# First batch of a spectral filter and its MLP on one core: filter rows in both partition halves, two load queues, another order of loads and sums

## The chip, the core and the metric

The kernel runs on one core of a Trainium2 chip. The metric is the time on the device in microseconds (us), from the program's start to its end: the median of three runs of the kernel before is 2878.39 us (2875.7 to 2886.1). The profile is one execution of it, with a span of 2877.8 us.

## The reference, cut to what matters

```python
batch, seq, dim = (8, 3008, 256)          # x; filt_r and filt_i have seq // 2 + 1 = 1505 rows
X = np.fft.rfft(x, axis=1)
y = np.fft.irfft(X * (filt_r + 1j * filt_i)[None], n=seq, axis=1)
# then each of the 8 * 3008 = 24064 rows of y, as a token of 256 numbers:
h = y @ w_in                              # 256 x 2048
g = h - np.tanh(h)
out = g @ w_out                           # 2048 x 256
```

The two weight matrices come as 64-bit floats; all else is float32.

## The kernel before

A transform of 3008 = 64 x 47 points is done in matmuls. Per batch there are four steps, with a trip through DRAM between them, because each step has another index in the partitions:

1. `first`: a 64-point transform. `x` is loaded, multiplied by `wf1` into PSUM (`pf`), copied by ACT (`a1`) and stored to `ct1`.
2. `middle`: 32 frequency slots, each a 47-point transform. `a2` comes from `ct1`; the matrices of four slots (`fg`) come in one load (`load_slots`); the product `pz` is multiplied by the filter (`fr` and `fi`), transformed back (`pe`), copied (`e1`) and stored to `ct2`.
3. `last`: the 64-point inverse. `e2` comes from `ct2`, and the product `pu` holds tokens, feature by token.
4. `up`, `shrink`, `down`: the MLP on groups of up to 512 tokens, in a form with seven products for eight. It needs sums and differences of weight blocks, made by POOL (G).

The batches go in units (0), (1, 2), (3, 4), (5, 6), (7). In the long main loop, `first` and `middle` of the next unit lie between the MLP steps of the present one. Unit 0 has nothing to hide behind: it is done in a part of its own, which this text calls the prologue. There the weights of five of the eight weight quarters are also converted from 64-bit words to float32 (`weights`), two jobs to a quarter, each in two stages with a `yield` after each, so that they are strung between the other steps.

Each engine issues its instructions in the order of the text, within each `manual_schedule` region. So an instruction that waits holds up all later ones of its engine, and a load that waits for its buffer holds up all later loads of its queue. SP issues most loads, ACT the stores of `a1` and `e1`, POOL the loads of the filter in the prologue.

The prologue, shortened (cuts are marked with `# ...`):

```python
nc.sync.dma_start(wf1, wf1_d)
xs = [load_x0(0, (0, 4, 8))]                 # x in three chunks of 8 of 24 steps
ws = weights(tiles0, range(5), 3)            # 10 jobs, 3 raw loads ahead; "raw" has 3 buffers
xs += [load_x0(1), load_x0(2)]
# ... pad to ct1
fts = {0: filters_of(0)}                     # POOL: memset, then 6 loads of filter rows
# ... gx cleared
next(ws)                                     # the first 3 raw loads
for c in range(3):
    for k, _ in enumerate(first0(xs[c], c)): # matmuls pf, ACT copies a1, ACT stores
        if k == 3 or k == 1 and c > 0:
            next(ws)                         # one stage of a weight job
G.dma_start(s2, s2_d)
fts[1] = filters_of(1)
a2 = {0: load_a2(0, 0, False)}
mats = {0: load_slots(0, pro), 1: load_slots(1, pro)}
next(ws)
double_filters(fts[0], 0)
turned(mats[0][1], gx[0])
for j in range(NK // 2):                     # 16 steps of two slots, c = j // 2
    # at even j: load a2[c + 1], mats[c + 2], fts[c + 2]
    # pz: 4 matmuls; back0 of step j - 1: 8 matmuls pe, ACT copy e1, store to ct2
    V.tensor_mul(uv, pz, ft[:, 0])
    V.tensor_mul(zs, pz, ft[:, 1])
    next(ws, None)
    # at odd j: double_filters and turned for c + 1
    if j == NK // 2 - 2:
        fs = first(1, z1)
        next(fs)                             # the first two x loads of unit 1
back0()
for _ in ws:
    pass
e2s[0] = load_e2(*groups[0])                 # all tokens of the first group
```

and what these call:

```python
def load_x0(c, cuts=(0, 8)):
    t = big([128, 8, DM], F32, "x0")
    for lo, hi in zip(cuts, cuts[1:]):
        for _, rows, r, n in halves(0, 8 * c + lo, hi - lo):   # partitions 0 to 63, then 64 to 127
            nc.sync.dma_start(t[rows, lo:lo + n, :], ...)

def filters_of(c, to=None):                  # t = filt[c % 3], [128, 2, 4, 256]
    # ... memset of t[32:64]
    for v, src in enumerate((filt_r, filt_i)):
        for row, m in ((0, LO), (LO, 16), (LO + 16, HI - 16)):  # 24, 16 and 7 partitions
            put(row, m, v, 0, n, src, ...)   # t[row:row + m, v, ...]: partitions 0 to 46

def double_filters(t, c):                    # partitions 64 to 127 get what 0 to 63 hold
    for v in range(2):
        ACT.copy(t[IM:128, v], t[0:IM, v])   # IM = 64

def weights(tiles, quarters, ahead):         # its loop over jobs k
    next(began[k])                           # stage 1: four DVE and two ACT operations on raw
    if k + ahead < len(jobs):
        began.append(start(k + ahead))       # SP: a raw load of 512 KB
    yield
    next(began[k])                           # stage 2: DVE writes wu or wd
    if k % 2:
        # four G.tensor_sub on the quarter just done
    yield
```

After the prologue, the main loop opens with `last` of group 0 (`pu`), and strings the 24 steps of `first` of unit 1, one x chunk each, between the MLP steps of unit 0.

Of the kernel before, what the change touches and what calls it, by code (L numbers as in the profile page):

```python
# [37 lines left out]

UNITS = [(0,), (1, 2), (3, 4), (5, 6), (7,)]
HALF = (NR + 1) // 2  # L40


def steps_of(unit):
# [97 lines left out]
def kernel(  # L141
# [81 lines left out]
    def weights(tiles, quarters, ahead):  # L223


        jobs = []
        for k in quarters:
            u = k % 4
            for h in range(2):
                if k < 4:  # L230
                    cols = slice(256 * u, 256 * u + 256)
                    src = bass.AP(tensor=moe_w_in.tensor, offset=128 * h * DFF + 256 * u,
                                  ap=[[DFF, 128], [DFF // 2, 2], [1, 256]])
                    dsts = [(slice(0, 256), wu[:, (0, 1)[h], cols], 1.0),
                            (slice(256, 512), wu[:, (6, 3)[h], cols], (1.0, -1.0)[h])]
                else:
                    t = 2 * u + h
                    cols = slice(128 * t, 128 * t + 128)
                    src = bass.AP(tensor=moe_w_out.tensor, offset=128 * t * DM,
                                  ap=[[DM, 128], [DFF // 2 * DM, 2], [1, DM]])  # L240
                    dsts = [(slice(0, 256), wd[:, 0:7:6, cols], 1.0),
                            (slice(256, 384), wd[:, 1, cols], 1.0),
                            (slice(384, 512), wd[:, 3, cols], -1.0)]
                jobs.append((src, dsts))

        def start(k):
            j = converted(tiles, *jobs[k], nc.sync)
            next(j)
            return j

        began = [start(k) for k in range(ahead)]
        yield
        for k in range(len(jobs)):
            next(began[k])
            if k + ahead < len(jobs):
                began.append(start(k + ahead))
            yield
            next(began[k])
            if k % 2:
                u = quarters[k // 2]  # L260
                w = (wu if u < 4 else wd)[:, :, 256 * (u % 4):256 * (u % 4) + 256]
                G.tensor_sub(w[:, 4], w[:, 6], w[:, 3])
                G.tensor_sub(w[:, 5], w[:, 4], w[:, 0])
                G.tensor_sub(w[:, 2], w[:, 1], w[:, 5])
                G.tensor_sub(w[:, 6], w[:, 0], w[:, 6])
            yield

    def halves(p, r, n):

# [132 lines left out]

    CHUNKS = [chunks_of(bs, CH) for bs in UNITS]

    def load_e2(p, c):
        r, n = CHUNKS[p][c]
        t = tr.tile([128, CH, DM], F32, tag="e2", bufs=2, name="e2")
        if len(UNITS[p]) == 2:
            nc.sync.dma_start(t[:, 0:n, :], dram(ct2[p], r * DM, [[RP * DM, 128], [1, n * DM]]))
        else:  # L410
            for _, rows, r_h, n_h in halves(p, r, n):
                nc.sync.dma_start(t[rows, 0:n_h, :],
                                  dram(ct2[p], r_h * DM, [[RP * DM, 64], [1, n_h * DM]]))
        return t
# [323 lines left out]
    psums = []  # L738

    def z1(name, shape):  # L740
        return psums[0].tile(shape, F32, tag="t", bufs=1, name=name)

    with tc.tile_pool(name="tr", bufs=2) as tr:
        with tc.tile_pool(name="pro", bufs=1) as pro, \
                tc.tile_pool(name="ps0", bufs=6, space=bass.MemoryType.PSUM) as ps0:

            def z0(name, shape):
                return ps0.tile(shape, F32, tag="z", bufs=6, name=name)

            def big(shape, dtype, name):  # L750

                return pro.tile(shape, dtype, tag="big", bufs=4, name=name)

            def load_x0(c, cuts=(0, 8)):
                t = big([128, 8, DM], F32, "x0")
                for lo, hi in zip(cuts, cuts[1:]):
                    for _, rows, r, n in halves(0, 8 * c + lo, hi - lo):
                        nc.sync.dma_start(t[rows, lo:lo + n, :],
                                          dram(x.tensor, r * DM, [[NR * DM, 64], [1, n * DM]]))
                return t  # L760

            def first0(xt, c):
# [24 lines left out]
            def filters_of(c, to=None):  # L787


                n = 4 if c < NK // 4 - 1 else 3  # L790

                def put(row, m, v, i, n_s, src, off, dims):
                    if to is None:
                        dst = t[row:row + m, v, i:i + n_s, :]
                    else:
                        dst = dram(to, ((row * 2 + v) * NK + 4 * c + i) * DM,
                                   [[2 * NK * DM, m], [DM, n_s], [1, DM]])
                    (G if to is None else nc.sync).dma_start(dst, dram(src.tensor, off, dims))

                if to is None:  # L800
                    t = filt[c % 3]


                    if c < 3:
                        G.memset(t[32:64], 0.0)
                    if n == 3:
                        G.memset(t[0:1, 1, 3], 0.0)
                for v, src in enumerate((filt_r, filt_i)):
                    for row, m in ((0, LO), (LO, 16), (LO + 16, HI - 16)):
                        sign = 1 if row < LO else -1  # L810
                        r0 = 4 * c + 1 + NQ * row if row < LO else NQ * (row - LO + 1) - 1 - 4 * c
                        put(row, m, v, 0, n, src, r0 * DM,
                            [[NQ * DM, m], [sign * DM, n], [1, DM]])
                    if n == 3:
                        put(v, LO - v, v, 3, 1, src, v * NQ * DM,
                            [[NQ * DM, LO - v], [DM, 1], [1, DM]])
                        put(LO, HI, v, 3, 1, src, NQ // 2 * DM,
                            [[NQ * DM, HI], [DM, 1], [1, DM]])
                return None if to is not None else t

            def double_filters(t, c):
                for v in range(2):
                    ACT.copy(t[IM:128, v], t[0:IM, v])
                if c == NK // 4 - 1:
                    ACT.dma_start(t[IM:IM + 1, 0, 3, :],
                                  dram(filt_r.tensor, SEQ // 2 * DM, [[DM, 1], [1, DM]]))
# [17 lines left out]
            with tc.manual_schedule():  # L844
                nc.sync.dma_start(wf1, wf1_d)
                V.memset(near_b, B)
                V.memset(exp_b, -896.0)
                xs = [load_x0(0, (0, 4, 8))]
                ws = weights(tiles0, range(5), 3)
                xs += [load_x0(1), load_x0(2)]  # L850

                pad = pro.tile([64, DM], F32, name="pad")
                G.memset(pad, 0.0)
# [2 lines left out]
                gx = [pro.tile([IM + RP, 4, RP2], F32, name=f"gx{k}") for k in range(2)]  # L856
                for t in gx:
                    G.memset(t[32:64], 0.0)
                next(ws)
                for c in range(3):  # L860
                    for k, _ in enumerate(first0(xs[c], c)):
# [2 lines left out]
                G.dma_start(s2, s2_d)  # L864
                fts[1] = filters_of(1)
                a2 = {0: load_a2(0, 0, False)}
                mats = {0: load_slots(0, pro), 1: load_slots(1, pro)}
                next(ws)
                double_filters(fts[0], 0)
                turned(mats[0][1], gx[0])  # L870
# [17 lines left out]
                for j in range(NK // 2):  # L888
# [23 lines left out]
                    if j == NK // 2 - 2:  # L912
                        fs = first(1, z1)
                        next(fs)
                back0()
                for _ in ws:
                    pass
                e2s[0] = load_e2(*groups[0])


        with tc.tile_pool(name="dn", bufs=2) as dn, \
                tc.tile_pool(name="ps", bufs=1, space=bass.MemoryType.PSUM) as ps:

            psums.append(ps)

            def tiles1(k, dtype, n):

# [25 lines left out]
            with tc.manual_schedule():  # L953
# [3 lines left out]
                for U in range(total + 2):  # L957
                    i, u = divmod(U, 4)
                    if U < total:
                        p, c = groups[i]  # L960
                        if c == 0 and u == 0:
                            units = 4 * len(CHUNKS[p])
                            steps, done = [], 0
                            if p + 1 < len(UNITS):
                                n_f = len(chunks_of(UNITS[p + 1], XH))
                                n_m = 2 * NK // (3 - len(UNITS[p + 1]))
                                steps = [0.01 * units + 1.36 * units * k / n_f for k in range(n_f)]
                                lo, hi = 1.6 * units, 5 * units - 17
                                steps += [lo + (hi - lo) * k / n_m for k in range(n_m)]
                                ms = None  # L970
                        if u == 0 and i + 1 < len(groups) and c + 1 < len(CHUNKS[p]):
                            e2s[i + 1] = load_e2(*groups[i + 1])
                        if u == 2 and i + 1 < len(groups) and c + 1 == len(CHUNKS[p]):
                            assert done == len(steps)
                            e2s[i + 1] = load_e2(*groups[i + 1])
                        if u == 0 and c + 1 == len(CHUNKS[p]) and p + 2 < len(UNITS):
                            fs = first(p + 2, z1)
                            next(fs)
                        if u == 2 and i + 1 < len(groups):
                            lasts = last(i + 1, z1)  # L980
# [93 lines left out]
```

## Time and profile before

| stretch of the span, us | what it holds | PE busy, us | mean granted TensorE clock | DMA share | GB/s |
|---|---|---|---|---|---|
| 50.47 to 115 (64.53 us) | the 16 steps of two slots | 54.27 | 0.84 | 0.77 | 195 |
| 123.2 to 220 (96.80 us) | first MLP steps, beside `first` of unit 1 | 83.27 | 0.92 | 0.55 | 172 |
| 220 to 2800 (2580 us) | main loop | 2541.70 | 1.00 | 0.28 | 67 |

A row of this kind gives, for a stretch of time, how long each engine was busy in it, the clock that the throttle granted to TensorE (1.00 is full), the mean busy share of the core's 16 DMA engines, and the bytes that they moved per time. The first `pz` matmul starts at 50.47 us, the last `pe` matmuls of unit 0 end at 115.26 us, and the first `pu` matmul, with which the main loop opens, starts at 123.21 us. Over the whole span PE is busy for 2743.9 us (95%), DVE for 1984.0 (69%), ACT for 1872.6 (65%) and POOL for 1747.4 (61%).

In the views of the trace, a timeline line gives start, length, engine, line of the kernel, operation, out<-in, shape, count and, in brackets, how long the engine had been idle and what ended that; a chain line gives start, length and what the chain of releases was in. SPq, ACTq and POOLq are the queues in which these engines issue DMAs.

### The profile page before, as it was taken

The numbers are of one execution on the slowest core, as the hardware profiler recorded it, in microseconds if no ns is written. First come the engines' busy times: TensorE is split into PE (matmuls) and PEld (weight loads), VectorE is DVE, ScalarE is ACT, GpSimd is POOL, SyncE is SP. The second block draws the span as 40 slices with busy tenths as digits, with TensorE's granted clock in tenths as the row PEclk, the third lists the DMA queues.
The fourth block names the chain that finished last, engine by engine and source line by source line (L and its number), as shares of the span: only waits on it lengthen the run. The fifth ranks groups of instructions, "written<-read, shape, count | busy, mean of one in ns | idle before, by whom it ended". The sixth has DMA issues, their size and how long they took to land.

```text
span 2877.8 us, 36465 instructions
## 1 busy us (share of the span) xinstructions
PE 2743.9 (95%) x12474; PEld 2274.9 (79%) x12474; DVE 1984.0 (69%) x2214; ACT 1872.6 (65%) x2460; POOL 1747.4 (61%) x1379
## 2 busy tenths in 40 slices
PE   4789999999999999999999999999999999999996
PEld 2567777888878787888877888888888888888885
DVE  3585666766776777766677777766777777777765
ACT  3466666666767676666666776666666666666663
POOL 4345777444677767645576777655476666555544
PEclk8899999999999999999999999999999999999998
DMA  9654443232233232222323233122233222110100
GB/s 241 164 185 128 116 107 90 66 94 77 70 78 84 75 74 53 56 82 83 87 70 76 68 78 81 36 46 66 51 75 81 53 55 56 24 28 16 25 12 16
DMA packets 328029, 217.46 MB, mean 76 GB/s; under 512 B 229053, under 2 KB 280373, under 8 KB 327642
## 3 DMA queue, kind: packets, MB, share of 16 engines
q1 hardware_dynamic: 273464, 162.00, 23.8%
q10 hardware_dynamic: 52418, 49.82, 5.7%
q0 software_dynamic: 1952, 3.22, 0.5%
q8 instruction: 100, 1.64, 0.2%
q14 instruction: 95, 0.78, 0.1%
HBM read 138.81 MB, written 79.17 MB: 76 GB/s over the span
## 4 chain that ended last, share of the span: by engine, by line
PE 68%; DVE 9%; ACT 8%; POOL 5%; issue 4%; DMA 3%; SPq 1%; ACTq 1%; DVEq 0%; POOLq 0%
PE o L577 27%; PE x L470 18%; PE z L470 8%; PE y L470 5%; PE pe L358 3%; PE pu L434 3%; PE pz L377 3%; DVE h L531 3%; ACT y L526 2%; PE pf L298 2%; ACT y L527 1%; POOL t L452 1%; ACT u L476 1%; DVE uv L392 1%; DVE h L506 1%
## 5 line engine op out<-in xcount | busy, mean ns | idle before, releaser
L577 PE MATMUL o<-t,wd 128*128 128x256 f32 (+2 forms) x3072 | 776.4, 375 | 1.8 <-POOL t L451 1.3
L531 DVE TENSOR_TENSOR h<-h,y 128x1024 f32<-128x1024 f32 (+2 forms) x384 | 587.9, 1531 | 253.2 <-ACT y L527 253.1
L449 POOL TENSOR_TENSOR t<-h 128x512 f32<-128x512 f32 (+2 forms) x192 | 240.1, 1251 | 739.9 <-DVE h L535 561.0
L577 PEld LDWEIGHTS o<-t,wd 128*128 128x128 f32 x3072 | 580.1, 190 | 74.5 <-POOL t L451 1.9
L470 PE MATMUL x<-tu,wu 128*128 128x256 f32 (+2 forms) x2304 | 589.4, 378 | 11.8 <-ACT u L476 10.9
L577 PE MATMUL o<-h,wd 128*128 128x256 f32 (+2 forms) x2304 | 581.3, 375 | 0.2 <-DVE h L535 0.2
L535 DVE SCALAR_TENSOR_TENSOR h<-sq,h 128x1024 f32<-128x1024 f32 (+2 forms) x384 | 566.9, 1476 | 21.2 <-ACT y L526 0.9
L470 PEld LDWEIGHTS x<-tu,wu 128*128 128x128 f32 x2304 | 428.5, 191 | 153.5 <-issue 74.1
L577 PEld LDWEIGHTS o<-h,wd 128*128 128x128 f32 x2304 | 430.8, 190 | 71.2 <-issue 18.3
L532 ACT ACTIVATE sq<-y,near_b 128x1024 f32<-128x1024 f32 (+2 forms) x384 | 435.5, 1134 | 5.5 <-DVE h L535 0.9
L526 ACT ACTIVATE y<-h 128x1024 f32<-128x1024 f32 (+2 forms) x384 | 400.0, 1042 | 14.9 <-ACT e L361 7.3
L476 ACT COPY s<-x 128x512 f32<-128x512 f32 (+2 forms) x192 | 110.8, 577 | 455.8 <-PE x L470 447.2
L527 ACT ACTIVATE y<-y 128x1024 f32<-128x1024 f32 (+2 forms) x384 | 399.3, 1040 | 12.2
L452 POOL TENSOR_TENSOR t<-t,h 128x512 f32<-128x512 f32 (+2 forms) x192 | 308.3, 1606 | 0.0
L476 ACT COPY u<-x 128x512 f32<-128x512 f32 (+2 forms) x384 | 219.5, 572 | 72.4 <-PE x L470 30.4
L393 POOL TENSOR_TENSOR zs<-zs,ft 128x512 f32<-128x512 f32 x112 | 165.9, 1481 | 143.0 <-ACT zs L391 142.9
L450 POOL TENSOR_TENSOR t<-h,t 128x512 f32<-128x512 f32 (+2 forms) x192 | 241.5, 1258 | 15.0
L451 POOL TENSOR_TENSOR t<-h 128x512 f32<-128x512 f32 (+2 forms) x192 | 249.3, 1298 | 0.0
L394 POOL TENSOR_TENSOR uv<-uv,zs 128x512 f32<-128x512 f32 x112 | 212.3, 1896 | 15.9 <-DVE uv L392 7.6
L470 PE MATMUL x<-ut,wu 128*128 128x256 f32 (+2 forms) x768 | 200.0, 383 | 11.8 <-DVE h L506 10.1
L470 PE MATMUL z<-tu,wu 128*128 128x256 f32 (+2 forms) x768 | 194.6, 376 | 1.3 <-DVE h L512 1.3
L486 DVE TENSOR_TENSOR h<-y,s 128x512 f32<-128x512 f32 (+2 forms) x192 | 130.3, 679 | 94.1 <-PE y L470 82.6
(112 smaller groups left out, 3299.1 us busy)
## 6 DMA issues: line engine op xcount, KB each, us to landing
a<-ct SPq DMA_DIRECT2D x64, 384.0 KB
ct<-e ACTq DMA_DIRECT2D x128, 192.0 KB
ft<-filt SPq DMA_DIRECT2D x96, 256.0 KB
out_dram<-ot SPq DMA_DIRECT2D x1408, 16.0 KB
ct<-a ACTq DMA_DIRECT2D x80, 256.0 KB
x_sb<-in_x_dram SPq DMA_DIRECT2D x69, 256.0 KB
e<-ct SPq DMA_DIRECT2D x33, 512.0 KB
fg<-fg SPq DMA_DIRECT2D x40, 392.0 KB
```

Of the source, the lines that this page charges most:

```text
L449: G.tensor_sub(t[0], b[0][1], b[0][0])
L450: G.tensor_sub(t[1], b[1][1], t[0])
L451: G.tensor_sub(t[2], b[1][1], b[0][1])
L452: G.tensor_sub(t[3], t[1], b[1][0])
L470: nc.tensor.matmul(bank[:, k], wu[:, q - 1, (2 * u + k) * 128:(2 * u + k + 1) * 128], rhs[q - 1], start=(first and k == 0), stop=True, ski ...
L476: ACT.copy(t, X)
L526: ACT.activation(y[k], ht[k], AF.Arctan, scale=S)
L527: ACT.activation(y[k], y[k], AF.Square)
L531: V.tensor_mul(ht[k], ht[k], y[k])
L532: ACT.activation(sq[k], y[k], AF.Square, bias=near_b, scale=A)
L535: V.scalar_tensor_tensor(out=ht[k], in0=sq[k], scalar=K, in1=ht[k], op0=ALU.add, op1=ALU.mult)
L577: nc.tensor.matmul(product(q), wd[:, q - 1, (2 * u + k) * 128: (2 * u + k + 1) * 128], rhs[q - 1][:, k], start=(u == 0 and k == 0 and q == ...
```

## The change

All of it concerns the prologue of unit 0, and how its end meets the main loop.

- **Filter rows:** `fr` still goes to partitions 0 to 46, `fi` now to 64 to 110. `double_filters` copies `fr` up and `fi` down. The six loads alternate between `fr` and `fi`, and the memset is cut into two of half the size.
- **x on two queues:** of each x load of unit 0, SP issues the part for partitions 0 to 63 and ACT that for 64 to 127.
- **Order of loads:** all x loads, then the matrices of slots 0 to 3 (`mats[0]`), then raw weights, of which two instead of three are now ahead; `raw` keeps three buffers. `mats[0]` was loaded behind `a2[0]`, after the whole of `first0`. The matrices of the prologue share four buffers with `a1`.
- **Sums:** the four POOL subtractions of a quarter come one stage later, after stage 1 of the next job.
- **Tokens in two parts:** of `e2` of group 0, rows 0 to 47 of each half are loaded at step 14 of 16, the other 16 rows after the last `back0`.
- **Three steps of `first` of unit 1** (`EARLY`) move from the main loop to the end of the prologue; the other 21 are spread over the same stretch of the main loop.

Cut to its core:

```diff
+EARLY = 3
 def weights(tiles, quarters, ahead):
             next(began[k])
+            if k and k % 2 == 0:
+                sums(quarters[k // 2 - 1])
             if k + ahead < len(jobs):
                 began.append(start(k + ahead))
             yield
             next(began[k])
-            if k % 2:
-                # the four G.tensor_sub, now in sums(u)
             yield
+        sums(quarters[-1])
+        yield
 def load_x0(c, cuts=(0, 8)):
-                    for _, rows, r, n in halves(0, 8 * c + lo, hi - lo):
-                        nc.sync.dma_start(t[rows, lo:lo + n, :],
+                    for h, rows, r, n in halves(0, 8 * c + lo, hi - lo):
+                        (nc.sync, ACT)[h].dma_start(t[rows, lo:lo + n, :],
 def filters_of(c, to=None):
-                        dst = t[row:row + m, v, i:i + n_s, :]
+                        dst = t[IM * v + row:IM * v + row + m, v, i:i + n_s, :]
-                        G.memset(t[32:64], 0.0)
+                        for v in range(2):
+                            G.memset(t[IM * v + 32:IM * v + 64, v], 0.0)
-                for v, src in enumerate((filt_r, filt_i)):
-                    for row, m in ((0, LO), (LO, 16), (LO + 16, HI - 16)):
+                for row, m in ((0, LO), (LO, 16), (LO + 16, HI - 16)):
+                    for v, src in enumerate((filt_r, filt_i)):
 def double_filters(t, c):
-                for v in range(2):
-                    ACT.copy(t[IM:128, v], t[0:IM, v])
+                ACT.copy(t[IM:128, 0], t[0:IM, 0])
+                ACT.copy(t[0:IM, 1], t[IM:128, 1])
 # the prologue
-                xs = [load_x0(0, (0, 4, 8))]
-                ws = weights(tiles0, range(5), 3)
-                xs += [load_x0(1), load_x0(2)]
+                xs = [load_x0(0, (0, 4, 8)), load_x0(1), load_x0(2)]
+                ws = weights(tiles0, range(5), 2)
+                mats = {0: load_slots(0, pro)}
                 next(ws)
                 # ... first0, s2, fts[1], a2[0]
-                mats = {0: load_slots(0, pro), 1: load_slots(1, pro)}
+                mats[1] = load_slots(1, pro)
                     if j == NK // 2 - 2:
                         fs = first(1, z1)
                         next(fs)
+                        e2s[0] = load_e2(*groups[0], None, slice(0, 48))
                 back0()
+                load_e2(*groups[0], e2s[0], slice(48, 64))
+                for _ in range(EARLY):
+                    next(fs)
                 for _ in ws:
                     pass
-                e2s[0] = load_e2(*groups[0])
```

(`z1`, which gives PSUM tiles to `first`, now takes them from the prologue's pool while that is open.)

## The prediction

> **What bounds the kernel now.** I first read the busy time of each engine in stretches of time. Its columns: the stretch; its length; busy time and count of PE, PEld, DVE, ACT, POOL; the granted clock; the busy share of the 16 DMA engines; GB/s.
>
> ```profile
> 0.00:20.00 20.00, 9.12 (x16) 3.54 (x16) 0.09 (x2) 3.53 (x5) 7.04 (x15) 1.00 0.91 201
> 20.00:40.00 20.00, 4.63 (x10) 1.64 (x10) 11.80 (x24) 9.94 (x17) 7.18 (x10) 0.76 0.99 326
> 40.00:60.00 20.00, 9.53 (x28) 7.19 (x29) 6.03 (x13) 3.99 (x7) 7.43 (x12) 0.56 0.91 196
> 60.00:80.00 20.00, 15.60 (x60) 10.60 (x59) 15.32 (x30) 14.31 (x22) 14.38 (x25) 0.91 0.94 257
> 80.00:100.00 20.00, 14.83 (x51) 9.88 (x50) 11.51 (x24) 10.40 (x17) 12.51 (x22) 0.80 0.90 222
> ```
>
> There are two regimes. From 220 to 2800 us PE is busy for 2541.7 of 2580 us, so the main loop is PE's, and the change adds and removes no PE work. In the first 100 us no compute engine is full, but the DMA engines are, at a share of 0.90 to 0.99, and at very different rates: 326 GB/s in one stretch and 196 to 257 in the others. What shortens the prologue should shorten the run one for one; nothing else can. Then the chain of waits, in order of time (start, length, what):
>
> ```profile
> 3.73 8.26 DMA x<-in_x_dram
> 12.01 10.53 DMA raw<-in_moe_w_in_dram
> 22.56 0.44 DVE conv L202
> ...
> 40.28 10.06 DMA fg<-fg
> 50.47 3.75 PE pz L898 x8
> ...
> 118.80 4.28 DMA e<-ct
> 123.21 2.06 PE pu L434 x8
> ```
>
> Read it as three links. ACT waits for the first raw block until 22.56 and does its remaining copies and stores of `first0` only then. The slot steps wait for the matrices until 50.47. The main loop waits for tokens until 123.21. Between 50.47 and 115 the chain jumps between engines, so I read ACT's timeline there, only the filter copies, of which there is one pair in every two steps, and the odd one out:
>
> ```profile
> 58.87 1.99 ACT L823 COPY filt<-filt 64x1024 f32<-64x1024 f32 x2 [0.61 <-ACT e L884]
> 65.17 1.99 ACT L823 COPY filt<-filt 64x1024 f32<-64x1024 f32 x2 [0.53 <-ACT e L884]
> 72.28 1.99 ACT L823 COPY filt<-filt 64x1024 f32<-64x1024 f32 x2 [0.47 <-ACT e L884]
> 81.79 1.99 ACT L823 COPY filt<-filt 64x1024 f32<-64x1024 f32 x2 [0.48 <-DMA filt<-in_filt_i_dram]
> 94.24 0.58 ACT L884 COPY e<-pe 96x512 f32<-96x512 f32 x1 [7.15 <-DMA ct<-e]
> 95.30 1.99 ACT L823 COPY filt<-filt 64x1024 f32<-64x1024 f32 x2 [0.47 <-ACT e L884]
> ```
>
> The intervals are 6.3, 7.1, 9.5 and 13.5 us. In the first, ACT is busy or issuing nearly throughout, so 6.3 us for two steps is ACT's floor and the rest is stalls. Last, the waits of SP's queue:
>
> ```profile
> SPq L195 <- DVE conv L209: 31.8, 4, 13.5
> SPq L412 <- DMA ct<-e: 20.5, 2, 14.7
> ```
>
> SP waits with a raw load until DVE has read the block three jobs before, and the `a2` and `fg` loads stand behind it.
>
> **What the Trainium skill says.** "SBUF — State Buffer", section "Door 1: The DMA port swizzle": partitions 0 to 63 reach only eight of the sixteen ports, 64 to 127 the other eight. The trace agrees with that picture: in the first 20 us SP's queue, nearly all 64-partition x loads, moves 3.38 MB in 75.7% of the time (223 GB/s while busy); from 20 to 40 us the same queue, now with raw loads over 128 partitions, moves 3.53 MB in 51.7% (341 GB/s). But the same page, section "Can I just issue two DMAs to hit both halves?", says that two DMAs at once on the two halves gained only 6%, and "DMA: Bandwidth & Descriptors", section "Issuing engines are not separate DMA queues", that loads from several engines share the same 16 DMA engines and save only issue time. No run here shows two such streams yet, so I take half of the gain in rate.
>
> **The change part by part.**
>
> *x on two queues, matrices and raw order.* By the first raw block's landing, `x` (3008 rows of 1 KB, 3.1 MB), `wf1` (0.13), the first filter loads (0.4), the block (0.5) and now the matrices (0.4) must be in: 4.5 MB. Data flow from about 3 us. At 223 GB/s that ends at 23 us, at 341 at 16 us; at 280, my choice, at 19 us, against 22.5. From the raw landing to the issue of `a2` it took 39.87 - 22.56 = 17.3 us, nearly all ACT's copies, conversions and DMA issues and the last store's landing; this stays, so `a2` goes out at about 36.5. Its 0.39 MB take 1.8 us at 223 GB/s and about 2 us to land (the shortest filter landing is 2.1 us). The matrices are there by then. `pz` can start at 41 instead of 50.5. Against that: `mats[0]` takes one of the four buffers of `a1` during `first0`, ACT has four more issues of about 0.6 us (ahead of its first data), and filters, matrices and `a2` of the following slots now all crowd into the same time. I count **8 us**, not 9.5.
>
> *Filters in two halves.* After 40 us there land about 2.7 MB of filter, 2.1 MB of raw (4 blocks), 3.2 of matrices (112 partitions, 64 of them low) and 3.1 of `a2` (96, 64 low). The low half gets 2.7 + 1.05 + 1.83 + 2.1 = 7.7 MB, the high one 3.5. With `fi` high it is 6.3 and 4.8. At 223 GB/s the low half takes 34.4 us before and 28.4 after: up to 6 us of DMA time. The copies of `double_filters` are the same in number and size (1.04 us each), so are the 52 load issues (0.53 us each on POOL), and two memsets of half size replace one of 1.8 us.
>
> *Two blocks ahead with three buffers* removes the wait on DVE: a raw load now goes into a buffer freed one job earlier. The load of `a2` that went out at 64.97 behind a raw load at 64.32 could go when `pz` of step 3 is done, at 61.2; PE stood for 3.39 us at 73.58 and for 3.42 us at 89.85 ("issue" in the view) before a `pz`, each some 9 us after such a load.
>
> *Sums later.* POOL issued the filter loads of slots 20 to 23 at 76.93, behind four subtractions that had waited for DVE for 5.13 us; now those loads come first. They take 6 to 9 us to land, so this helps at just the two longest intervals.
>
> Together: the four intervals named and the two after them (to 102.15 and 108.47, so 6.85 and 6.3) hold 11.7 us above 6.3 each. PE needs 16 x 2.6 = 42 us at full clock, ACT 8 x 6.3 = 50, and the DMA, with about 14 MB to move in less time than now, stays near its limit. I take half of the stalls away: **6 us**.
>
> *Tokens in two parts, EARLY.* The last store goes out at 115.92; 2.1 us for it, two issues, 4.28 us for 0.5 MB. The second part has only 0.13 MB, so about 2 us less. But the third early step needs an x load that SP issues behind it, and PE does that step before `pu`, so most of this is lost again at the start of the main loop. The gain is that three steps (each 0.86 us of PE at full clock) leave the main loop's start for a time when PE stood for 7.9 us, and that the 2.8 us which PE waited at 137.73 for an x load go. **4 us.**
>
> Sum: 8 + 6 + 4 = 18 us; 2878.4 - 18 = 2860.
>
> **Rivals.** (1) *The loads don't gain from the halves*, as the skill's 6% says: the DMA engines stay as full as now and only order changes. Then the first part gives some 4 us, the slot steps 3, the end 4: about 2867. For it: a share over 0.9 throughout. Against: raw loads and `a1` stores together reached 341 and 330 GB/s, so the engines can do more when ports are spread. (2) *All stalls vanish*, ACT becomes the bound of the slot steps: 10 + 11 + 6 = 27 us, 2851. Against: stores to `ct2` waited up to 13 us to land in a crowd of loads, and the crowd gets denser. (3) *A new wait takes the place*: ACT stuck with a store for want of an `a1` buffer, filter loads of slots 4 to 7 now needed at 48 us and landing no earlier, or PE stuck behind the third early step. Then 2872 to 2880. (4) The main loop's start is bound by DVE's late conversions (PE 83.3 of 96.8 us busy from 123.2 to 220) and gives nothing back, or swallows some: a loss of at most a few us.
>
> **Range and chances.** The prologue ends at 123 us, and 2% of the time is 57.6 us, more than all its stalls. So faster by over 2% is next to impossible; slower by 2% would need a stall of half the prologue. The range reaches from rival 2 with a little more to rival 3: 2846 to 2874.
>
> **What will show it.** Right: the 0 to 20 us stretch rises from 201 to 260 GB/s or more; first raw landing at 17 to 21 us; first `pz` at 39 to 44 us with the wait on `a2`, no longer on `fg`; filter copies at intervals of 6.3 to 8 us; no wait of SP on DVE's reads of raw in the prologue; first `pu` near 108 us; a main loop of unchanged length from there, less about 4 us. Wrong: the same GB/s with the same share (rival 1); ACT idle for stores or filters (rival 3); a `pu` start earlier by far more than the time (rival 4).

## The result and the profile after

The changed kernel takes 2880.26 us (median of six runs, 2878.08 to 2881.76) against 2880.43 us for the kernel before on the same chip (2875.7 to 2886.1): a ratio of 0.9998, with a 95% interval of 0.9985 to 1.001. The prediction was 2860 us, with a range of 2846 to 2874. The 18 us that were to be gained did not come.

The busy time of each engine in stretches, for the changed kernel (columns as before: stretch, length, PE, PEld, DVE, ACT, POOL, clock, DMA share, GB/s; a packet counts whole where it starts, so a share can pass 1):

```profile
0.00:20.00 20.00, 11.77 (x20) 4.33 (x20) 0.09 (x2) 3.63 (x5) 7.09 (x16) 1.00 0.94 248
20.00:40.00 20.00, 2.86 (x6) 0.96 (x6) 11.95 (x24) 10.96 (x19) 8.56 (x13) 0.62 0.94 313
40.00:60.00 20.00, 15.18 (x54) 11.07 (x55) 13.75 (x24) 6.67 (x10) 13.46 (x23) 0.78 1.04 246
60.00:80.00 20.00, 13.60 (x42) 8.95 (x41) 11.48 (x23) 12.33 (x18) 8.53 (x15) 0.74 0.94 246
80.00:100.00 20.00, 17.24 (x73) 11.38 (x71) 18.36 (x37) 15.19 (x25) 11.99 (x20) 1.00 0.76 211
```

The first line went from 201 to 248 GB/s, the third from 196 to 246, while the others fell by 11 to 13: the prologue did start earlier and the DMA engines did move more. Pieces of the chain of waits (start, length, what):

```profile
5.59 15.56 DMA raw<-in_moe_w_in_dram
...
43.59 8.18 DMA filt<-in_filt_i_dram
...
58.71 4.96 DMA filt<-in_filt_i_dram
...
110.93 3.30 DMA x_sb<-in_x_dram
114.36 2.06 PE pf L304 x2
```

`fg`, which held the first `pz` before, is gone from the chain. The first raw block (landed at 21.15, before at 22.54) and filter loads are still there; new is, at the end, a load of `x` for the third early step. On PE's timeline the start and the end of the prologue:

```profile
43.02 3.75 PE L915 MATMUL pz<-a,fg 94*128 94x256 f32 x8 [9.60 <-DMA a<-ct]
...
114.36 2.04 PE L304 MATMUL pf<-x_sb,wf_sb 128*128 128x512 f32 x2 [6.05 <-DMA x_sb<-in_x_dram]
117.08 2.08 PE L447 MATMUL pu<-s_sb,e 128*128 128x128 f32 x8 [0.68 <-ACT a L305]
```

So the first `pz` starts 7.45 us earlier than before (50.47), and the first `pu` 6.1 us earlier (123.21). The main loop opened with a lead of 6 us, and the program ended with none. To find where the lead went I compared one recurring instruction in both traces, the first ACT copy (`s<-x`) of every MLP step. MLP steps are numbered from 0 here; "the seventh" in the expectations quoted below is step 7 of this numbering, and later expectations call the same one the eighth.

| start of | before, us | after, us | after minus before |
|---|---|---|---|
| first `pu` | 123.21 | 117.08 | -6.1 |
| MLP step 1 | 141.93 | 134.78 | -7.2 |
| MLP step 3 | 180.32 | 172.22 | -8.1 |
| MLP step 4 | 199.27 | 193.74 | -5.5 |
| MLP step 5 | 215.34 | 215.42 | +0.1 |
| MLP step 7 | 246.22 | 247.59 | +1.4 |
| MLP step 11 | 319.64 | 321.02 | +1.4 |

From step 7 to the last, step 191, the offset stays at 1.0 to 1.6 us. So 2600 us of main loop are untouched, and between 172 and 248 us a lead of 8 us turns into a lag of 1.4. SP's timeline in that stretch (`filt` from `in_filt` here is a copy from DRAM to DRAM, which arranges the filter for the later units):

```profile
182.53 0.77 SPq L814 DMA_DIRECT2D filt<-in_filt_r_dram  x1
189.94 0.72 SPq L814 DMA_DIRECT2D filt<-in_filt_i_dram  x1
190.70 1.38 SPq L814 DMA_DIRECT2D filt<-in_filt_r_dram  x1
194.62 0.58 SPq L814 DMA_DIRECT2D filt<-in_filt_i_dram  x1
...
196.92 0.39 SPq L283 DMA_DIRECT2D x_sb<-in_x_dram  x1
```

ACT's and PE's, beside it:

```profile
187.80 0.37 ACTq L306 DMA_DIRECT2D ct<-a  x1
...
192.44 0.37 ACTq L306 DMA_DIRECT2D ct<-a  x1
```

```profile
201.38 1.16 PE L304 MATMUL pf<-x_sb,wf_sb 128*128 128x512 f32 x2 [4.23 <-DMA x_sb<-in_x_dram]
```

SP issues nothing for 6.6 us, goes on 2 us after ACT's store of `a1`, stops again, goes on 2 us after the next such store, and only then comes to the `x` load. PE waits 4.23 us for that load. A filter copy has nothing to do with `a1`. But in the built program the DMAs issued by SP and by ACT complete on the same eight semaphores in turn, and each waits for the one eight places before it; those issued by POOL complete on eight others. So a copy on SP waits for a store on ACT, the `x` loads stand behind the copy in SP's order, PE waits for `x`, and the next `a1` that ACT can store waits for PE.

The waits from the first `pu` to 300 us (total, times, longest), PE's and then those of SP's queue, in the kernel before:

```profile
PE pf L298 <- DMA x_sb<-in_x_dram: 4.6, 4, 2.8
```

```profile
SPq L798 <- DMA ct<-a: 15.1, 6, 5.7
```

and in the kernel after:

```profile
PE pf L304 <- DMA x_sb<-in_x_dram: 6.9, 3, 4.2
```

```profile
SPq L814 <- DMA ct<-a: 25.5, 7, 6.6
```

(The 13.0 us that the expectation of a_pool gives for the main loop hold the 6.05 us of the third early step as well, which stand ahead of the first `pu`; 6.9 are the main loop's.) The wait is in the kernel before too; the change lengthens it.

PE's waits for `x` are only part of the loss. From the start of step 3 to that of step 7, before and after (columns as above):

```profile
180.32:246.22 65.90, 61.75 (x255) 48.02 (x254) 49.27 (x57) 41.27 (x57) 30.46 (x26) 0.97 0.51 152
172.22:247.59 75.37, 65.14 (x251) 50.54 (x250) 49.71 (x57) 40.94 (x55) 32.77 (x30) 0.91 0.44 127
```

The stretch grew by 9.5 us: 4.6 are PE's waits for `x` (6.4 against 1.8), 1.5 a wait for an ACT copy of the MLP (3.8 against 2.3), and 3.4 are PE's busy time, 65.1 us for 251 matmuls against 61.8 for 255, at a granted clock of 0.91 against 0.97. Why the clock was lower no run here tests.

Two theories of the lost lead were to be tried: this queue of SP, and, as the prediction's fourth rival had it, DVE's late weight conversions (DVE is busy for 17.83 of the 20 us from 180 to 200, in the kernel before for 19.43).

### The profile page after: what moved, and what is told of

It reads as the page before. It is cut to its first block, busy times and chain, and to the rows that moved or that the text cites. A ratio compares the mean times of both kernels' runs of the same rounds, so it can differ in the third digit from the quotient of the medians.

```text
span 2879.3 us, 36469 instructions
## 1 busy us (share of the span) xinstructions
PE 2748.1 (95%) x12474; PEld 2278.9 (79%) x12474; DVE 1989.3 (69%) x2214; ACT 1872.2 (65%) x2460; POOL 1743.4 (61%) x1382
## 4 chain that ended last, share of the span: by engine, by line
PE 69%; DVE 9%; ACT 8%; POOL 5%; issue 4%; DMA 3%; SPq 1%; ACTq 0%; DVEq 0%; POOLq 0%
PE o L590 27%; PE x L483 18%; PE z L483 8%; PE y L483 5%; PE pe L364 3%; PE pu L447 3%; DVE h L544 3%; PE pz L383 3%; ACT y L539 2%; PE pf L304 2%; ACT y L540 1%; POOL t L465 1%; ACT u L489 1%; DVE uv L398 1%; DVE h L519 1%
## 5 line engine op out<-in xcount | busy, mean ns | idle before, releaser
L483 PE MATMUL x<-ut,wu 128*128 128x256 f32 (+2 forms) x768 | 200.0, 383 | 12.2 <-DVE h L519 10.7
L483 PE MATMUL z<-ut,wu 128*128 128x256 f32 (+2 forms) x768 | 194.8, 376 | 0.0
```

The lines of the kernel that those rows point to most:

```text
L483: nc.tensor.matmul(bank[:, k], wu[:, q - 1, (2 * u + k) * 128:(2 * u + k + 1) * 128], rhs[q - 1], start=(first and k == 0), stop=True, ski ...
```

## The experiments

A trace is one execution, and a kernel's runs spread by some 5 us either way (a_pool: 2869.24 to 2878.43). So the traces serve to place a loss, and the ratios of repeated runs to size it. All leads are against the one trace of the kernel before. b_pool, whose prologue is that of the kernel before, shows how far traces differ: first `pz` at 49.27 us (before 50.47), slot steps of 67.5 us (64.8), `pu` at 124.73 (123.21). Six kernels with the same work up to the last `pe` (after, a_pool, a_few, a_order, a_early0, a_few_e2) have the first `pz` at 42.67 to 44.01 us and slot steps of 61.5 to 63.6. Only a_low, a_oneq, a_noraw and a_e1x4 have one time each and are read by their traces.

### Who takes the lead in the main loop

**a_pool and b_pool**: the filter copies of the main loop issued by POOL, in the kernel after and in the kernel before.

```diff
-(G if to is None else nc.sync).dma_start(dst, dram(src.tensor, off, dims))
+G.dma_start(dst, dram(src.tensor, off, dims))
```

> The kernel after the change, with the filter copies to DRAM in the main loop (56 of them, for the later units) issued by POOL instead of SP. Theory A: the lead of 6 us at the first pu, and the three steps of unit 1 done early, are lost between 180 and 245 us because the x loads of unit 1 stand behind these copies in SP's queue, which itself waits for stores of ACT. Then PE's waits for x_sb in the main loop (13.0 us in all after the change, 4.2 and 2.2 of them after 200 us) all but vanish, the seventh MLP step starts at 240 us or earlier instead of 247.6, and the run is 6 to 10 us faster than before, ratio 0.9966 to 0.998. Theory B: DVE with the late weight conversions sets the pace until about 240 us; then the seventh step stays at 246 to 248 us and the ratio at 0.999 to 1.001. Theory C: POOL is needed for the sums of the MLP and 56 issues of 0.55 us hold it up; then PE waits for t of POOL appear and the run is slower than before.

> The kernel before the change, with the same filter copies issued by POOL. Theory A: the start of the main loop is not bound by SP here any more either, but begins 6 us later and has three more steps to do; it gains less than the changed kernel with the same edit, so that the two differ by 6 to 9 us; this one is 0 to 4 us faster than before. Theory B: no change against before, and none against the changed kernel with this edit.

Measured: a_pool 2874.36 us, ratio to before 0.9982 (0.9975 to 0.9988); b_pool 2877.03, 0.9993 (0.9985 to 1.0001). So a_pool stays just short of the gain expected by theory A, and the two differ by 2.7 us, not 6 to 9. In a_pool the lead is 7.7 us at `pu`, 7.3 at step 5 and 9.8 at step 7. The waits of a_pool, same stretch, PE's and then SP's queue:

```profile
PE pf L304 <- DMA x_sb<-in_x_dram: 0.6, 1, 0.6
```

```profile
SPq L283 <- PE pf L304: 53.0, 13, 7.7
```

PE's wait for `x` in the main loop fell from 6.9 to 0.6 us; the third early step still waits 5.17 us ahead of `pu`. SP now waits 53 us, but for free `x` buffers: it is ahead of PE, which costs nothing. In the kernel before the same edit brings little: after 200 us its PE had waited only 1.8 us for `x`.

**a_few**: the 56 copies of the main loop become ten large ones, still on SP. The loop over slots gives way to six copies like this (three row blocks, `fr` and `fi`) and four for the last slot:

```diff
-for c in range(NK // 4):
-    filters_of(c, filt_d)
-    yield
+nc.sync.dma_start(
+    dram(filt_d, (row * 2 + v) * NK * DM, [[2 * NK * DM, m], [DM, NK - 1], [1, DM]]),
+    dram(src.tensor, r0 * DM, [[NQ * DM, m], [sign * DM, NK - 1], [1, DM]]))
```

> The kernel after the change, with the filter copies to DRAM in the main loop done in 10 DMAs over all slots instead of 56 over four slots each, still on SP. Theory A: SP has 46 issues of some 0.75 us less and far fewer waits for stores of ACT; the x loads come in time, the seventh MLP step starts by 241 us, and the run is 6 to 10 us faster than before. Theory B: no change. A third outcome: ten large copies (up to 0.74 MB each) crowd the DMA queues at once and x loads land late behind them: PE waits for x_sb remain, in a shorter stretch.

Measured: 2874.56 us, 0.9983 (0.9976 to 0.9989), 5 us faster than before where 6 to 10 were expected. Lead 6.5 us at `pu`, 6.1 at step 5, 8.7 at step 7. The bytes are the same as in the kernel after, only the number of SP's DMAs is not, and the time is that of a_pool: two quite different cures of the same queue.

**a_nolate**: the six late weight conversions of the main loop are left out, and three quarters of `w_out` are zero. This leaves out part of the computation; its time only tells what the conversions cost.

```diff
-late, copies = weights(tiles1, range(5, 8), 2), filters_d()
+late, copies = iter(()), filters_d()
```

> The kernel after the change without the six late weight conversions; it leaves out three of the four quarters of w_out, whose blocks are zero instead, so it computes less than the reference. All matmuls stay. Theory B (DVE's conversions set the pace of the first MLP steps): the first six steps take 15 us each instead of 11, 18, 19.5, 21.5, 21.7, the seventh starts before 230 us and the run is 10 us or more faster than before. Theory A: the steps up to the fourth are a few us faster, but the x loads behind the copies still hold PE at 195 to 245 us, and the run gains 0 to 4 us.

Measured: 2863.61 us, 0.9945 (0.9931 to 0.9959). Lead 4.9 us at `pu`, 15.2 at step 4, 15.6 at step 7. So in this kernel the conversions cost some 10 us in the stretch: PE is not its sole bound, as the fourth rival said. Not all of that need be DVE's: with the conversions go raw loads of SP's queue, whose waits for stores of `a1` at the copies fall from 25.5 to 13.8 us. But they were in the kernel before as well, so they alone do not explain a *new* loss; a_pool and a_few keep them and keep the lead.

**a_order**: the change also turned the order of these copies (row block by row block instead of all `fr`, then all `fi`); here the old order is restored in the main loop.

```diff
-for row, m in ((0, LO), (LO, 16), (LO + 16, HI - 16)):
-    for v, src in enumerate((filt_r, filt_i)):
+for v, src in enumerate((filt_r, filt_i)):       # for the copies in DRAM alone
+    for row, m in ((0, LO), (LO, 16), (LO + 16, HI - 16)):
```

> The kernel after the change with the 56 copies of the main loop in the order of before (three of fr, then three of fi); the loads of the prologue keep the new order. If the alternation of the copies is what makes SP's stall larger than before the change, the fifth MLP step takes 16 to 18 us instead of 21.7 and the lead of 6 us lives on to the end, 2873 to 2876 us. If the order is no matter, everything is as after the change, 2878 to 2881 us.

Measured: 2883.52 us, 1.0007 (0.9997 to 1.0016); lead 5.9 us at `pu`, gone at step 5 (0.0). The order plays no part.

**a_early0**: the kernel after with no early steps, all else kept.

```diff
-EARLY = 3
+EARLY = 0
```

> The kernel after the change with EARLY = 0: all 24 steps of unit 1 stay in the main loop, at the positions they had before the change; filter copies in 56 pieces on SP, as in before and after. If the three early steps and the new spacing of the other 21 are what makes SP's stall swallow the lead between the fifth and the eighth MLP step, pu starts at about 111 us and the lead at the eighth step (246.2 us before) stays at 4 us or more, total 2872 to 2876. If the stall is there for any early start, the lead falls to 2 us or less by the eighth step, total 2877 to 2881.

Measured: 2872.59 us, 0.9974 (0.9967 to 0.9982), an interval wholly below that of the kernel after. `pu` starts at 112.48. The lead is 10.7 us there, 10.2 at step 5, 10.8 at step 7 and 10.5 at the end. Its waits:

```profile
PE pf L304 <- DMA x_sb<-in_x_dram: 4.2, 4, 2.7
```

```profile
SPq L814 <- DMA ct<-a: 16.4, 6, 7.6
```

These are the sizes of the kernel before (4.6 and 15.1). So the three early steps, the part that was to bring 4 us, took away everything that the rest brought: 4.6 us at once, since `pu` stands behind the third step's `x` load, and the remainder later, through SP's queue. Without them the lead of the prologue reaches the end.

### What limits the slot steps

The 16 slot steps, from the first `pz` to the last `pe`, took 64.8 us before and 63.6 after, where 6 us less had been predicted. With the other traces of the same work (67.5 in b_pool; 61.5 to 63.6 after) the gain is 1.2 to 6 us, 3 by the means.

**b_halves** is the kernel before with only `fr` and `fi` in different halves; **a_low** is the kernel after with only that undone.

```diff
-dst = t[row:row + m, v, i:i + n_s, :]
+dst = t[IM * v + row:IM * v + row + m, v, i:i + n_s, :]
-for v in range(2):
-    ACT.copy(t[IM:128, v], t[0:IM, v])
+ACT.copy(t[IM:128, 0], t[0:IM, 0])
+ACT.copy(t[0:IM, 1], t[IM:128, 1])
```

> The kernel after the change with the filter rows back in partitions 0 to 46 for both fr and fi; order of issues, memsets and all else as after the change. If the two halves matter for the rate (the prediction's step), the filter loads are slower: their queue falls below the 222 GB/s while busy that it shows now, and the 16 slot steps take 5 to 6 us longer than the 63.5 us from first pz to last pe. If they don't, both stay within 1.5 us.

> The kernel before the change with fr and fi in different halves of the partitions and nothing else of the change. The changed kernel without the halves had 69.1 us of slot steps against 63.6. If the halves act by themselves, the slot steps of before (64.8 us) fall to 59 to 61, pu starts 4 to 5 us earlier, and the eighth step is earlier by that less what SP's stall takes (it cost before 2 us): 2874 to 2878 us. If the halves help only where the loads are crowded at the start, the slot steps stay above 63 us.

Measured: a_low 69.1 us of slot steps against 63.6 (5.5 more), time 2889.26 beside 2880.12 for before; b_halves 60.8 against 64.8 (4.0 less), 2876.61 us, 0.9991 (0.9981 to 1.0001). The halves bring 4 to 5.5 us in the slot steps, either way round (by the other traces up to 7.6), close to the 6 that were predicted for DMA time. In a_low the queue of the filter loads moves 198 GB/s while busy in the slot steps, in the kernel after 223. In b_halves, a kernel with no early steps, the lead of 5.6 us at `pu` is 4.1 at step 7 and 3.9 at the end.

**a_noraw**: from the fourth weight job of the prologue on, the raw blocks of the first three are used again: seven of ten loads left out (3.7 MB, of which 2.7 MB in the slot steps), so the weights are not the reference's.

```diff
-t = tiles("raw", I64, n)
-queue.dma_start(t, src)
+t = kept.get(len(made) % 3)          # a raw tile of the first three jobs
+if t is None:                        # only for those three
+    t = tiles("raw", I64, n)
+    queue.dma_start(t, src)
```

**a_e1x4**: the slot steps' stores to `ct2` go out of four buffers instead of two, the other two being those of `a1`.

```diff
-e1 = tr.tile([RP2, 2, DM], F32, tag="e1", bufs=2, name="e1")
+e1 = tr.tile([RP2, 2, DM], F32, tag=("e1", "a1")[j % 2], bufs=2, name="e1")
```

> The kernel after the change with only the first three of the ten raw weight blocks of the prologue loaded; the seven other conversions run on these three again, so the weights are not those of the reference. 3.7 MB of about 14 MB less to move in the slot steps. If the DMA engines' total load holds the slot steps back, they fall from 63.5 us to 57 or less and the stores to ct2 land in time. If not, they stay above 61 us.

> The kernel after the change with four buffers for e1 in the prologue (two of them those of a1 of the main loop, idle there). If ACT, waiting for an e1 buffer until a store to ct2 has landed (11.4 us of such waits in the slot steps), is what holds the slot steps back, these waits vanish and the 63.5 us fall by 6 us or more. If the load of the DMA engines is behind it, the waits move to the filter rows or to a2 and the steps gain 3 us or less.

Measured: slot steps of 56.5 us in a_noraw and 59.8 in a_e1x4 (2875.38 and 2874.58 us). a_noraw is clear. a_e1x4 lies between its two expected outcomes, and of a_few_e2 and a_few_e2x4 below, which differ in the same buffers, the slot steps are 61.5 and 61.1 us: 59.8 lies below the spread of the six traces, 0.4 within it, so what four buffers bring there stays open. What both edits act on is seen on ACT's timeline of the kernel after:

```profile
50.70 1.04 ACT L839 COPY filt<-filt 64x1024 f32<-64x1024 f32 x1 [0.57 <-DMA filt<-in_filt_r_dram]
...
61.48 0.58 ACT L901 COPY e<-pe 96x512 f32<-96x512 f32 x1 [5.47 <-DMA ct<-e]
...
62.59 1.04 ACT L839 COPY filt<-filt 64x1024 f32<-64x1024 f32 x1 [0.53 <-ACT e L901]
...
71.38 0.58 ACT L901 COPY e<-pe 96x512 f32<-96x512 f32 x1 [3.49 <-DMA ct<-e]
```

The filter copies, one pair for two steps, start at 50.70, 62.59, 72.43, 79.10, 85.34, 92.03 and 99.96: intervals of 11.9, 9.8, 6.7, 6.2, 6.7 and 7.9 us. The stalls of before (9.5 and 13.5 at 72 to 95 us) are gone from where they were, and there are new ones in the first two intervals, where ACT waits for a buffer until the store made at 50.16 has landed, 11 us later. The bytes tell more. In its slot steps the kernel before moves 195 GB/s x 64.53 us = 12.6 MB, the kernel after 13.9 MB: 0.9 MB of loads that used to arrive ahead of the first `pz` now arrive behind it, and the first 0.4 MB of the tokens come before the last `pe`. What they cost is an estimate. In a_noraw 2.7 MB less in the slot steps gave 7.0 us, 2.6 us per MB, and b_halves, which has the halves but only 12.9 MB, takes 2.8 us less than the kernel after. By a_noraw's rate the 1.3 MB are 3.4 us, at the 219 GB/s of the kernel after 5.9: most of what the halves bring.

### Two queues for x

**a_oneq**: the kernel after with SP issuing both halves of every `x` load.

```diff
-(nc.sync, ACT)[h].dma_start(
+nc.sync.dma_start(
```

> The kernel after the change with all x loads of unit 0 issued by SP. If the two queues are what brought the first pz from 50.5 to 43.0 us, it goes back by 4 us or more, and the first 20 us move 200 to 215 GB/s instead of 248. If it was the earlier load of the matrices and the later raw loads, pz stays within 1.5 us of 43.

Measured: 2878.23 us; first `pz` at 45.45 us (43.02 with two queues, 50.47 before), first raw block at 23.42, 205 GB/s from 0 to 20 us. This lies between the two expected outcomes: two queues give 2.4 of the 7.45 us (1.4 to 2.8 by the traces named above), and the rest of the change the other 5, most likely the matrices ahead, since PE's wait for `fg` is gone. The DMA queues of the first 20 us (packets, MB, share of the 16 engines' time), a_oneq and then the kernel after:

```profile
q1 hardware_dynamic: 869, 3.50, 76.5%
```

```profile
q1 hardware_dynamic: 855, 2.63, 49.0%
q10 hardware_dynamic: 690, 1.87, 34.9%
```

3.50 MB in 76.5% of 20 us are 229 GB/s while busy; with the halves on two queues it is 268 for both together. But these bytes hold raw and matrix loads too, over more partitions. From 3 to 15 us, when by the bytes moved these queues still carry `x` and `wf1` alone, the thirteen traces with two queues have 248 to 264 GB/s while busy and the four with one (before, b_pool, b_halves, a_oneq) 230 to 239: some 9%. The Trainium skill ("SBUF — State Buffer", section "Can I just issue two DMAs to hit both halves?") has 6% for two such DMAs, which is near it.

### Putting the findings together

Four versions of the kernel after, each with the ten large copies: **a_few_e2** has two early steps, which need no `x` load beyond the two already issued; **a_few_e2x4** also the four buffers of a_e1x4; **a_more4** and **a_more47** moreover convert six and seven weight quarters in the prologue instead of five, so that fewer are left for the main loop.

```diff
-EARLY = 3
+EARLY = 2
```

```diff
-ws = weights(tiles0, range(5), 2)
+ws = weights(tiles0, range(6), 2)
-late, copies = weights(tiles1, range(5, 8), 2), filters_d()
+late, copies = weights(tiles1, range(6, 8), 2), filters_d()
```

> The changed kernel with ten large filter copies and two early steps of unit 1 instead of three. The third early step waits 5.4 to 6.1 us for an x load that SP can issue only behind the last token load. If that wait sits in front of the first pu, pu starts about 3 us earlier (113.5 instead of 116.7 us), one step of 0.86 us goes back to the main loop, and the run is 1 to 3 us faster than with three (2874.6): ratio to before 0.9973 to 0.998. If the main loop's start swallows it, the eighth MLP step stays at 237.6 us and the run at 2874 to 2875 us.

> The same with four buffers for e1 in the prologue. With three early steps and the old copies the buffers brought the first pu from 117.1 to 113.5 us. If leads of the prologue now reach the end of the run, this one is another 3 to 4 us faster than with two buffers, near 2869 us, ratio 0.9955 to 0.997. If not, both have the same time.

> The same as the run with two early steps and four e1 buffers, and six instead of five weight quarters converted in the prologue, so four late conversions instead of six in the main loop. DVE stands idle from 103 to 122 us, so the two conversions should cost little there. The kernel without any late conversion gained 17 us at the eighth step over the changed one, so a conversion costs the main loop's start up to 2.8 us: 2 to 5 us less than without this, near 2866 us. If the gain without conversions was SP's stall in another shape, 0 to 1 us.

> The same with seven weight quarters in the prologue and two late conversions. Two more conversions of 4 us each end at about 116 us, after the first pu could start, and ACT has their operations ahead of its copies of pu: pu is up to 3 us later, the main loop's start another 2 to 5 us shorter. 2862 to 2868 us; not faster than with six if ACT's order costs what DVE gains.

| kernel | us | ratio to before (95%) | lead at `pu` | at step 7 |
|---|---|---|---|---|
| a_few_e2 | 2870.18 | 0.9966 (0.9954 to 0.9978) | 10.8 | 12.0 |
| a_few_e2x4 | 2864.11 | 0.9943 (0.9929 to 0.9957) | 12.9 | 16.3 |
| a_more4 | 2863.97 | 0.9939 (0.9925 to 0.9952) | 11.0 | 16.1 |
| a_more47 | 2865.94 | 0.9941 (0.9927 to 0.9954) | 10.0 | 15.2 |

One early step less gives 4.3 us of lead at `pu` over a_few, the four buffers 2.1 more. Together they make a version 0.57% faster than the kernel before, whose time the kernel after has. a_few_e2 and a_few_e2x4 are both faster than was expected. Moving weight conversions on top of that brought nothing more, where 2 to 5 us were expected: the prologue pays for them (`pu` 1.9 us later in a_more4, 3.0 in a_more47, where PE then waits 10.09 us more for an ACT copy before the second `pu`). No early steps at all together with few copies and four buffers was not tried.

The kernels by how the lead changes from `pu` to step 7 (plus is lost):

| kernels | early steps | copies on SP | lost from `pu` to step 7, us |
|---|---|---|---|
| after, a_order, a_oneq, a_e1x4, a_low, a_noraw | 3 | 56 | 7.5, 7.2, 4.9, 4.4, 4.1, 4.7 |
| a_early0 | 0 | 56 | -0.1 |
| b_halves (kernel before) | 0 | 56 | 1.5 |
| b_pool (kernel before) | 0 | none | -2.5 |
| a_pool | 3 | none | -2.1 |
| a_few, a_few_e2, a_few_e2x4 | 3, 2, 2 | 10 | -2.1, -1.2, -3.4 |

Every kernel with three early steps, many copies on SP and all late conversions loses 4 us or more there, and none of the others does. Taking away either the early steps or the copies is enough. a_nolate, with both but without the late conversions, gains 10.7 us there, so in it the loss cannot be told apart from what leaving out conversions brings.

## Why the prediction was wrong, by its own steps

- **x on two queues, matrices and raw order: 8 us.** Right: 7.45, with PE's wait now on `a2` and no longer on `fg`; one third of it is the second queue, two thirds the rest, by PE's waits the order of loads. The rate fell a little short (248 GB/s, not 260), and the raw block landed at 21.2 us, not 19.
- **Filters, raw ahead, sums: 6 us.** The mechanism was right and the term mis-sized: 1.2 us in this pair of traces, some 3 by all. The halves give 4 to 5.5 us by themselves. But the working counted the same bytes into the stretch before and after, although the first step starts it 7.45 us earlier. The 1.3 MB that move in cost most of what the halves bring (3.4 to 5.9 us, an estimate); a_noraw shows that the loads set the pace. The two raw loads ahead did not remove the wait on DVE: SP's waits on DVE's reads of raw became shorter (31.8 and 9.2 us for two operations before, 14.6 and 7.9 after) but did not go. The later sums were not tried by themselves.
- **Tokens in two parts, EARLY: 4 us.** The first half was right: without early steps the time from the last `pe` to `pu` is 5.5 us instead of 7.9, the 2 us that were worked out. EARLY had the wrong sign. The text saw that the third step waits for `x` ahead of `pu`, and set the three steps' 2.6 us of PE against it; it did not ask what SP's queue does in the main loop with the remaining 21 steps. PE's wait at 137.73 did go, and waits of 4.23 and 2.22 us at 201 and 239 came instead, with a lower clock beside them.
- **"One for one; nothing else can".** This is the step that failed most: the text took the main loop for PE's alone from its start. Of 6 us at `pu` nothing was left at step 7. Without EARLY the sentence holds: 10.7 us at `pu`, 10.5 at the end, and 7.5 by repeated runs (0.9974).
- **The rivals.** Rival 1 came in part: the stretch moved 248 GB/s, not 201, but `x` alone gained some 9%, and 5 us of the first term came without the second queue. Rival 3 came too, with PE stuck behind the third early step and ACT held by stores, to `ct2` and not of `a1`. Rival 4 is what happened: "a `pu` start earlier by far more than the time". Its size, "a loss of at most a few us", was wrong, 7.5 us, and so was its cause alone: the conversions are dear (a_nolate), but the new loss is SP's queue.

What stays open: that 21 steps, spread over the stretch of 24, sit further apart beside the same number of copies, and so let SP's wait reach PE, is argued from the timelines; the runs show only that both the early steps and the copies on SP are needed. Nor does a run separate the time in which SP issues the copies from its waits at them; that is read from the timelines and the waits. Two early steps with all copies on SP were not tried. In some traces (a_pool, a_order, a_low, a_more4, a_more47) another 2 to 3 us are lost from step 188 on, in the last part of the kernel; no run here looks into that.

## What to carry to other kernels

A lead gained in one part of a kernel is worth only what the next part lets through: follow one recurring instruction through both traces, and the place where its offset changes is the place to look. When work is moved to an earlier time its loads move too, so count the bytes of a stretch anew before crediting it with a faster transfer. And look at what stands ahead of a critical load in its engine's order: an unrelated DMA can wait there for another engine's store, if both complete on the same semaphores.

## What was not expected of the hardware

- Loads of `x` on two queues, one for each half of the partitions, moved 248 to 264 GB/s while busy from 3 to 15 us, on one queue 230 to 239, in thirteen and four traces: a real gain, though worth only some 2 us here.
- A store of 192 KB to `ct2` in the midst of loads took 11 us to land (issued at 50.16, waited for until 61.48, at a DMA share of 1.05); the last one of the prologue, at a share of 0.43, took 2.15 us.
- The same four MLP steps took PE 3.4 us more busy time where it also waited more (granted clock 0.91 against 0.97): the loss was larger than the waits.
